# Block 0's Mish loop reordered and block 1's recurrence chain spread over more places, in a fused delta-rule, Mish-MLP and mixture kernel

## The chip, the cores and the metric

One core of a Trainium2 chip runs the whole program. The metric is device microseconds of one execution, the median of a few runs; the time before is 2250.83 us (three runs, 2248.86 to 2260.82).

## The reference, cut to what matters

Three layers follow one another. A delta-rule recurrence runs over 768 positions of 4 batches x 8 heads (head size 48); its output is 3072 tokens of 384 columns. An MLP with 2048 hidden columns and Mish follows, and then a mixture of 8 experts of 1024 hidden columns, weighted by a matrix that eight row and column normalisations balance.

```python
for t in range(S):
    y[:, :, t] = einsum('bhd,bhde->bhe', q[:, :, t], state)
    v_old = einsum('bhde,bhd->bhe', state, k_n[:, :, t])
    state = state + beta * einsum('bhd,bhe->bhde', k_n[:, :, t], v[:, :, t] - v_old)
...
h = x @ w_in;  x = (h * tanh(softplus(h))) @ w_out          # Mish MLP
...
P = exp(x @ w_gate - max); 8 times: P /= rows; P /= columns; P *= N / E
out = sum over e of P[:, e] * (relu(x @ w1[e]) @ w2[e])
```

## The kernel before

Every float32 matrix is split into a high part (fp32r) and a low part, the remainder, so each product is three matmuls: high by high, low by high, high by low.

The first two layers are done in six blocks of 512 tokens (`NBLK`; c is the block). A block has 16 *Mish units*, one for each 128 hidden columns, and blocks 0 and 1 (`c < NE0`) have 8 *expert units* of expert 0 behind them. In Mish unit f TensorE does `m_first` (9 matmuls, line 314, into one of two PSUM buffers), ScalarE does Mish (`m_a`, line 1302 or 1304) and a rounded copy, the high part (`m_c`, line 1310), VectorE or GpSimd subtracts to get the low part (line 1312), and TensorE does `m_second` (9 matmuls, line 1323), two units later. An expert unit is alike with Relu: lines 314, 328, 329 and 338.

Block 0 also decodes the MLP's weights, which arrive as 64-bit words. For each chunk of 128 columns ScalarE does `begin_decode` (line 193, and line 210 in three chunks of four), VectorE does a sign and a shift step (lines 199 and 204; in the fourth chunk line 196 as well), ScalarE rounds to the high part (`rounded`, line 257) and VectorE subtracts (line 276, in `convert`). A weight chunk is then stored to memory, to be loaded again in the next blocks, and its buffer is refilled.

The recurrence of the next block (a *chain*) is woven into the units of this one. Its 64-position triangular systems are inverted in halves: `lane_in` transposes on VectorE, 60 short elimination products and adds on VectorE (lines 1096 and 1102, in the queue `eq`), `st_lane_out` (two transposes, lines 1111 and 1112), matmuls `st_m1` (line 1139) and `st_m2` (line 1154) with copies, and the copies of `st_place` (lines 1121 and 1123). Then come stages z, w, s, y (lines 1181, 1203, 1221, 1237), twice, each with a VectorE or ScalarE step behind it. `st_g` (line 1033) builds the products of the block after the next.

All order is written out by hand, and each engine takes its instructions in that order. The list `MARKS` names the places of a block: s0 to s15 (Mish units), f1 to f4 (the boundary), s16 to s23 (expert units). `PLACES` says where each chain stage goes; `fill(us)` pops eliminations from `eq` until their written costs (0.2 us + size / 960 each) reach `us`; `rate` lets each `vec` instruction pop some too; `drain_elim` does what is left. In blocks from 1 on a place issues its first two stages ahead of the unit's `m_first` and the others behind; in block 0 stages go in pairs ahead of the unit's first product, behind it, and behind its second product.

The other experts run behind the six blocks.

Of the kernel before, what the change touches and what calls it, by code (L numbers as in the profile page):

```python
# [9 lines left out]
F32R = mybir.dt.float32r  # L10
# [75 lines left out]
def delta_mish_sinkhorn_kernel(  # L86
# [137 lines left out]
    def begins(n):  # L224
        while begun[0] < n:
            begin_decode(begun[0])
# [582 lines left out]
    if True:  # L809
# [355 lines left out]
        def m_run(*parts):  # L1165
            for i in range(16):
                for one, _ in parts:
                    one(i)
            return [post for _, post in parts]
# [136 lines left out]
        def m_c(u):  # L1306
            p = hps.pop(u) if u < U1 else mi_x[u % 2]
            h = mi_p.tile([128, 512], F32R, tag="gh", name="gh")
            l = mi_p.tile([128, 512], F32R, tag="gl", name="gl")
            nc.scalar.activation(out=h, in_=p, func=AF.Copy)  # L1310
            eng = nc.vector if u < U1 else nc.gpsimd
            eng.tensor_tensor(out=l, in0=p, in1=h.bitcast(F32), op=ALU.subtract)  # L1312
            gh[u], gl[u] = h, l

# [57 lines left out]
        if True:  # L1372
# [88 lines left out]
            m1a()  # L1461
            warm(2)
            m2a = m_run(st_m2(0, 0, (0,)))[0]
            st_place(0, 0, (0, 2))
            m2a()
            warm(3)
            w = [st_w(0, t) for t in range(2)]
            m1b()
            w[0]()
            m2b = m_run(st_m2(0, 1, (0, 64)))[0]  # L1470
            w[1]()
            s0 = st_s(0, 0)
            m2b()
            warm(1)
            s1 = st_s(0, 1)
            st_place(0, 1, (0, 1, 2, 3))
            s0()
            s1()
            begins(3)
            warm(2)  # L1480
            z = [st_z(0, 2)]
# [40 lines left out]
        def drain_decode():  # L1522
# [2 lines left out]

        two = lambda *marks: [m for m in marks for _ in range(2)]
        PLACES = [
            (22, [24, 24, 24, 24, 24, 24, 25, 25, 25, 25, 25, 25, 26, 26], 16, [26, 26, 27, 27],
             [26, 26, 26, 26, 27, 27, 27, 27], 18, 26, None),
            (8, spread(11, 26, 1, 16), 1, [11, 11, 13, 15], spread(12, 19, 1, 8), 1, 27, 21),  # L1530
        ] + [
            (0, two(3, 5, 7, 8, 9, 11, 12, 13), 0, [3, 3, 6, 7], two(4, 5, 7, 8), 0, 15, 9),
        ] * 4
# [3 lines left out]
        def window(c):  # L1537
# [18 lines left out]
            if nxt < NBLK:  # L1556
                m0, at = PLACES[c][0:2]
                rest[MARKS[m0]].append(drain_elim)
                if c == 0:
                    rest[MARKS[m0]].append(lambda: nc.vector.memset(seed_sb, 0.0))  # L1560
                rest[MARKS[m0]].append(lambda: st_lane_out(nxt))
                if c == 0:
                    rest[MARKS[m0]].append(lambda: nc.gpsimd.memset(seed_sb, 0.0))
                    for t in range(4):
                        rest[MARKS[m0 + t // 2]].append(lambda t=t: prep_v(1, t))
                    for i in range(8):
                        rest[MARKS[m0 + i // 2]].append(lambda t=i // 2, w=1 + i % 2: mask_p(1, t, (w,)))
                if c == 0:
                    m = MARKS[m0 + 1]
                    for make in (st_m1, st_m2):  # L1570
                        for hf in range(2):
                            pe[m].append(lambda hf=hf, make=make: m_run(make(nxt, hf))[0])
                    for hf in range(2):
                        rest[m].append(lambda hf=hf: st_place(nxt, hf, (0, 2)))
                        pe[m].append(lambda t=hf: st_z(nxt, t))
                    ch = [lambda f=f, t=NG * j + g: f(nxt, t) for f, j in (
                        (st_w, 0), (st_s, 0), (st_z, 1), (st_w, 1), (st_y, 0), (st_s, 1), (st_y, 1)
                    ) for g in range(NG)]
                else:
                    for hf in range(2):  # L1580
                        late[MARKS[m0 + 1]].append(lambda hf=hf: m_run(st_m1(nxt, hf))[0])
                        rest[MARKS[m0 + 2]].append(lambda hf=hf: st_place(nxt, hf, (0, 2)))
                        late[MARKS[m0 + 2]].append(lambda hf=hf: m_run(st_m2(nxt, hf))[0])
                    ch = chain_list(nxt)
                assert len(at) >= len(ch)
                for p, stage in zip(at, ch):
                    pe[MARKS[p]].append(stage)
                if c == 0:
                    pe[MARKS[27]][0:0] = [lambda: lambda: None] * 2
# [26 lines left out]
        if True:  # L1616
            banks[:] = [0, [A1, A1]]
            for c in range(NBLK):
# [40 lines left out]
                for f in range(U1 + (3 if c < NE0 else 2)):  # L1659
                    m = MARKS[f]  # L1660
                    posts = side_pe(m, 0)
                    if f < U1:
                        ready(b + f)
                        m_first(b + f)
                        if not c:
                            converts(min(U1, f + 2))
                            if f == 0:
                                for n in (3, 4):
                                    wslots[n] = wpool.tile([128, 2, 2, DM], F32R, tag=f"w{n}", name=f"w{n}")
                            if f == 3:  # L1670
                                wslots.append(late_p.tile([128, 2, 2, DM], F32R, tag="e2", name=f"w{NS1 - 1}"))
                    if 1 <= f <= U1:
                        m_a(b + f - 1)
                        m_c(b + f - 1)
                    if f == 0 and 0 < c <= NE0:
                        y0_second(b - 1)
                    if f == 1 and 0 < c <= NE0:
                        y0_done(c - 1)
                    if f == 5:
                        flush_xr()  # L1680
                    if f == 2 or not c:
                        banks[1] = [A1, A1, (ps_o1, "o3")]
                    if c >= NE0 and split and f >= U1:
                        run(*(split[0:2] if f == U1 else split[2:]))
                    if f == U1 + 1:
                        m_second(b + U1 - 1)
                        x2_done(c)
                    side_rest(m, posts)
                    if 2 <= f <= U1:
                        m_second(b + f - 2)  # L1690
                    fill((0.5 if f < U1 else 2.0) if not c else 3.2 if c >= NE0 and f > 8 else 2.0)
                    if f < U1:
                        if not c:
                            decodes(min(U1, f + 3))
                            if f + 2 < U1:
                                rounded(f + 2)
                            begins(min(U1, f + 4))
                        if ncvt[0] >= U1:
                            conversions(b + f)
                if c >= NE0:  # L1700
                    continue
                side_rest("f4", side_pe("f4", 0))
                fill(2.0)
                banks[1] = [A1, A1]
                for f in range(U1, NU):
                    u = b + f
# [6 lines left out]
                        e_relu(u - 1)  # L1713
                    side_rest(f"s{f}", posts)
                    if f > U1 or not c:
                        fill(2.4 if c == 0 else 3.2)
                    if f > U1 + 1:
                        y0_second(u - 2)
                    if not c:
# [193 lines left out]
```

## Time and profile before

| what | value |
|---|---|
| median of three runs | 2250.83 us |
| the profiled execution: its own time, and its span | 2253.7 us, 2251.9 us |
| TensorE busy | 2169.7 us (96%) |
| VectorE, ScalarE, GpSimd busy | 1394.4, 701.8 and 655.0 us |
| mean granted TensorE clock | 0.98 of full speed |

The busy shares are means over stages with different limits. In the first four of the 40 slices (225 us) TensorE is busy seven tenths, in the next three eight to nine, and the granted clock is below nine tenths in four of these seven; from then on TensorE is busy nine tenths or more. A granted clock of 1.00 is 2.4 GHz and 0.50 is 1.2 GHz; a value between them is a mean over a stretch that had both.

### The profile page before, as it was taken

How to read it: one execution, taken by the hardware profiler on the slowest of the kernel's cores; microseconds unless marked ns; L12 is line 12 of the kernel's file. 1: busy time of each engine (PE TensorE's matmuls, PEld its weight loads, DVE VectorE, ACT ScalarE, POOL GpSimd, SP SyncE). 2: the span in 40 equal slices, each digit the busy share in tenths (PEclk: the TensorE clock that was granted, in tenths of full speed). 3: DMA queues.
4: the chain of work that ended last, by engine and by line, in shares of the span. 5: the costliest groups of instructions: out<-in, count | busy, mean ns of one | idle time of the engine just before them, and what ended most of it. 6: DMA issues, size and time to landing. Idle time of an engine off the chain costs nothing.

```text
span 2251.9 us, 34773 instructions
## 1 busy us (share of the span) xinstructions
PE 2169.7 (96%) x14150; PEld 1788.8 (79%) x14150; DVE 1394.4 (62%) x2296; ACT 701.8 (31%) x1218; POOL 655.0 (29%) x514
## 2 busy tenths in 40 slices
PE   7777989999999999999999999999999999999999
PEld 5656877888888788888888888888888888888887
DVE  7667554655641257777777676666666666666665
ACT  6553332323332445333333322122222222112122
POOL 4104333243422756677878710000000000000000
PEclk8898998999999999999999999999999999999999
DMA  6566542635345535655555435443534454344441
GB/s 183 210 211 202 179 149 100 202 128 188 127 156 197 196 117 198 252 194 194 211 184 213 162 129 157 151 170 125 173 126 146 154 155 157 124 159 135 173 146 47
DMA packets 123648, 370.35 MB, mean 164 GB/s; under 512 B 9440, under 2 KB 51232, under 8 KB 123232
## 3 DMA queue, kind: packets, MB, share of 16 engines
q1 hardware_dynamic: 122912, 367.74, 47.8%
q8 instruction: 111, 1.82, 0.3%
q10 hardware_dynamic: 576, 0.39, 0.1%
q14 instruction: 49, 0.40, 0.1%
HBM read 274.15 MB, written 93.95 MB: 163 GB/s over the span
## 4 chain that ended last, share of the span: by engine, by line
PE 85%; DVE 7%; ACT 2%; issue 2%; POOL 1%; DMA 1%; SPq 0%; DVEq 0%; ACTq 0%; POOLq 0%
PE s L677 33%; PE b L610 30%; PE psh L314 7%; PE x L1323 6%; PE y L338 1%; DVE lane L1102 1%; PE psa L1033 1%; DVE t L1096 1%; PE psa L1181 1%; PE psa L1203 1%; PE psa L1237 1%; PE psa L1154 1%; DVE us L889 1%; PE psa L1139 1%; DVE lane L1066 1%
## 5 line engine op out<-in xcount | busy, mean ns | idle before, releaser
L610 PE MATMUL b<-gx,gw 128*128 128x512 f32 x3036 | 795.3, 390 | 0.1
L617 DVE TENSOR_TENSOR gt<-b,gt 128x512 f32<-128x512 f32 x644 | 435.9, 689 | 459.4 <-PE b L610 429.6
L610 PEld LDWEIGHTS b<-gx,gw 128*128 128x128 f32 x3036 | 568.2, 188 | 118.5 <-ACT gt L619 0.9
L677 PE MATMUL s<-gh,gw 128*128 128x512 f32 x2208 | 622.8, 390 | 1.3 <-DVE gy L720 1.1
L652 ACT ACTIVATE gh<-gt 128x512 fp32r<-128x512 f32 x368 | 232.8, 633 | 933.9 <-DVE gt L646 931.5
L677 PEld LDWEIGHTS s<-gh,gw 128*128 128x128 f32 x2208 | 413.6, 188 | 87.7 <-DVE gy L720 1.5
L677 PE MATMUL s<-gl,gw 128*128 128x512 f32 x1104 | 326.8, 390 | 0.0
L314 PE MATMUL psh<-x,w 128*128 128x512 f32 x1008 | 271.8, 417 | 39.1 <-DVE gl L1312 26.4
L646 DVE SCALAR_TENSOR_TENSOR gt<-gt,gp 128x512 f32<-128x512 f32 x336 | 278.0, 827 | 4.5
L314 PEld LDWEIGHTS psh<-x,w 128*128 128x128 f32 x1008 | 194.2, 199 | 91.1 <-DVE gl L1312 31.8
L677 PEld LDWEIGHTS s<-gl,gw 128*128 128x128 f32 x1104 | 206.9, 188 | 42.8
L655 POOL TENSOR_TENSOR gl<-gt,gh 128x512 fp32r<-128x512 f32 x128 | 185.8, 1458 | 78.5 <-ACT gh L652 71.8
L655 DVE TENSOR_TENSOR gl<-gt,gh 128x512 fp32r<-128x512 f32 x240 | 164.5, 685 | 37.0 <-ACT gh L652 36.8
L1312 POOL TENSOR_TENSOR gl<-x,gh 128x512 fp32r<-128x512 f32 x80 | 102.9, 1288 | 252.1 <-ACT gh L1310 226.4
L1323 PE MATMUL x<-gh,w 128*128 128x512 f32 x576 | 154.6, 405 | 0.7 <-ACT gh L1310 0.7
L550 POOL TENSOR_TENSOR gx<-gxr,gx 128x768 fp32r<-128x768 f32 x18 | 33.3, 1848 | 407.3 <-ACT gx L549 407.3
L481 POOL TENSOR_TENSOR gw<-gr,gw 128x640 fp32r<-128x640 f32 x70 | 117.5, 1681 | 68.2 <-ACT gw L491 66.4
L1323 PEld LDWEIGHTS x<-gh,w 128*128 128x128 f32 x576 | 109.6, 194 | 25.3 <-issue 1.4
L997 POOL TENSOR_TENSOR kq<-kq,mask_sb 64x256 f32<-64x256 f32 (+1 forms) x80 | 67.3, 841 | 77.9 <-ACT kq L992 73.6
L1304 ACT ACTIVATE x<-psh 128x512 f32<-128x512 f32 x80 | 47.6, 596 | 133.5 <-PE psh L314 123.7
L1323 PE MATMUL x<-gl,w 128*128 128x512 f32 x288 | 82.6, 395 | 3.2 <-POOL gl L1312 3.2
L481 POOL TENSOR_TENSOR gw<-raw,gw 128x384 fp32r<-128x384 f32 x70 | 73.4, 1069 | 7.3 <-ACT gw L513 7.3
(206 smaller groups left out, 1946.4 us busy)
## 6 DMA issues: line engine op xcount, KB each, us to landing
gw<-wg SPq DMA_DIRECT2D x57, 1280.0 KB, 8.0
w<-wd SPq DMA_DIRECT2D x88, 768.0 KB, 4.4
gw<-wg SPq DMA_DIRECT2D x57, 768.0 KB, 5.1
wg<-gw SPq DMA_DIRECT2D x29, 1280.0 KB, 6.1
wg<-gw SPq DMA_DIRECT2D x29, 768.0 KB, 5.1
wd<-w SPq DMA_DIRECT2D x24, 768.0 KB, 5.7
gr<-in_w_dram SPq DMA_DIRECT2D x35, 384.0 KB, 3.2
raw<-in_w_dram SPq DMA_DIRECT2D x35, 384.0 KB, 3.6
```

The costliest lines, as they stand in the source:

```text
L314: mm(ps, lhsT=wi(u, pw, kc), rhs=(xh, xl)[px][:, kc, :], start=(n == 0), stop=(n == 3 * KD - 1))
L481: nc.gpsimd.tensor_tensor(out=w[:, 1, lo:hi], in0=r, in1=w[:, 0, lo:hi].bitcast(F32), op=ALU.subtract)
L610: mm(ps, lhsT=w[:, pw, i * 128:i * 128 + 128], rhs=x[:, px, j, :], start=(n == 0), stop=(n == last))
L617: add = lambda o, i: nc.vector.tensor_tensor(out=t[:, o], in0=ps, in1=t[:, i], op=ALU.add)
L646: nc.vector.scalar_tensor_tensor(out=t, in0=t, scalar=0.0, in1=pbs[u, e][:, o:o + 512], op0=ALU.max, op1=ALU.mult)
L652: nc.scalar.activation(out=h, in_=t, func=AF.Copy)
L655: return lambda: eng.tensor_tensor(out=l, in0=t, in1=h.bitcast(F32), op=ALU.subtract)
L677: mm(o[k], lhsT=w[:, pw, at:at + 128], rhs=hids[s, z][ph], start=(start and new and n == 0), stop=(end and not new and n == 2))
L997: nc.gpsimd.tensor_tensor(out=o, in0=o, in1=mask_sb[p, None, :].to_broadcast([64, hs.stop - hs.start, CH]), op=ALU.mult)
L1304: nc.scalar.activation(out=mi_x[u % 2], in_=hps.pop(u), func=AF.Mish)
L1312: eng.tensor_tensor(out=l, in0=p, in1=h.bitcast(F32), op=ALU.subtract)
L1323: mm(x2ps[c][k], lhsT=wo(u, pw, k * 128, k * 128 + 128), rhs=(h, l)[pg], start=(f == 0 and n == 0), stop=(f == U1 - 1 and n == 2))
```

## The change

- Block 0's Mish units: `m_a` and `m_c` of the unit before now come ahead of `converts`, and the `rounded` call at the unit's end is gone, so the rounding of a chunk is issued inside `convert`, one unit later than before.
- Eliminations: block 0 pops 1.0 us a Mish unit (before 0.5), less at the boundary, and none inside `x2_done`; block 1 pops 3.2 a Mish unit (before 2.0) and 2.4 an expert unit (before 3.2).
- Block 1's chain, woven into block 0's expert units: it starts at s16 (before s18) and takes seven places, s17 to s23, two stages at a time.
- Block 1: `st_g` of block 3 two at a time in s12 to s15 (before one at a time in s12 to f4), and block 3's eliminations enter the queue at f1 (before s17). In Mish units 0 to 8 the low part of h is subtracted on VectorE (before GpSimd).
- Start: all four `st_place` copies of the first half on ScalarE (before two on VectorE), and the second half's `st_m2` behind the stages s.

```diff
-            eng = nc.vector if u < U1 else nc.gpsimd
+            eng = nc.vector if u < U1 or place[u][0] == 1 and place[u][1] < 9 else nc.gpsimd
...
-            st_place(0, 0, (0, 2))
+            st_place(0, 0, (0, 1, 2, 3))
             m2a()
             warm(3)
             w = [st_w(0, t) for t in range(2)]
             m1b()
             w[0]()
-            m2b = m_run(st_m2(0, 1, (0, 64)))[0]
             w[1]()
             s0 = st_s(0, 0)
-            m2b()
             warm(1)
             s1 = st_s(0, 1)
             st_place(0, 1, (0, 1, 2, 3))
+            m2b = m_run(st_m2(0, 1, (0, 64)))[0]
             s0()
             s1()
+            m2b()
...
         PLACES = [
-            (22, [24, 24, 24, 24, 24, 24, 25, 25, 25, 25, 25, 25, 26, 26], 16, [26, 26, 27, 27],
-             [26, 26, 26, 26, 27, 27, 27, 27], 18, 26, None),
-            (8, spread(11, 26, 1, 16), 1, [11, 11, 13, 15], spread(12, 19, 1, 8), 1, 27, 21),
+            (20, [22, 22, 23, 23, 23, 23, 24, 24, 24, 24, 24, 24, 25, 25, 26, 26], 16, [24, 25, 26, 27],
+             [25, 25, 25, 25, 26, 26, 27, 27], 18, 26, None),
+            (8, spread(11, 26, 1, 16), 1, [11, 11, 13, 14], two(12, 13, 14, 15), 1, 27, 16),
...
-                        if not c:
-                            converts(min(U1, f + 2))
...
                     if 1 <= f <= U1:
                         m_a(b + f - 1)
                         m_c(b + f - 1)
+                    if not c and f < U1:
+                        converts(min(U1, f + 2))
...
                         m_second(b + U1 - 1)
+                        rate(0.6 if c else 0.0)
                         x2_done(c)
+                        rate(0.6)
...
-                    fill((0.5 if f < U1 else 2.0) if not c else 3.2 if c >= NE0 and f > 8 else 2.0)
+                    if c < NE0:
+                        fill((3.2 if c else 1.0) if f < U1 else 2.0 if f < U1 + 2 else 0.5)
+                    else:
+                        fill(3.2 if f > 8 else 2.0)
                     if f < U1:
                         if not c:
                             decodes(min(U1, f + 3))
-                            if f + 2 < U1:
-                                rounded(f + 2)
                             begins(min(U1, f + 4))
...
-                fill(2.0)
+                fill(0.5)
...
-                        fill(2.4 if c == 0 else 3.2)
+                        fill(2.4)
```

In the code that is left out of the diff, block 0's `st_m1` moves to place s17 and its `st_m2` to s18, with `st_place` beside `st_m1`, and the stage z of the first pair becomes part of the list that `PLACES` places.

## Rows read from the trace of the kernel before

**Rows 1.** Windows by stage of blocks 0 and 1: stretch, length, busy us per engine (instructions), PEclk, DMA share.

```profile
68.49:178.12 109.63, 82.51 (x354) 62.05 (x352) 71.69 (x107) 55.88 (x85) 1.90 (x2) 0.89 0.65 225
178.12:263.87 85.75, 69.92 (x1089) 61.03 (x1089) 51.03 (x99) 25.48 (x50) 38.49 (x38) 0.90 0.53 178
263.87:303.17 39.30, 37.39 (x168) 30.64 (x166) 34.99 (x67) 14.19 (x25) 17.15 (x10) 1.00 0.69 216
303.17:318.26 15.09, 10.51 (x151) 8.80 (x152) 8.96 (x17) 4.80 (x8) 1.28 (x1) 0.66 0.20 67
...
360.96:375.89 14.93, 12.83 (x170) 11.24 (x169) 5.07 (x10) 5.93 (x14) 7.52 (x10) 0.66 0.30 107
375.89:419.26 43.37, 40.70 (x348) 36.21 (x344) 35.97 (x86) 6.26 (x11) 0.00 (x0) 0.96 0.43 145
419.26:2251.90 1832.64, 1817.73 (x10236) 1502.62 (x10233) 1126.94 (x1779) 527.32 (x849) 535.41 (x400) 1.00 0.47 161
```

**Rows 2.** Waits of TensorE from 0 to 430 us: total us, times, longest.

```profile
PE psh L314 <- DVE gl L1312: 26.4, 13, 4.5
PE psh L314 <- DVE hl L329: 8.2, 1, 8.2
PE psa L1154 <- issue: 6.1, 3, 4.3
PE psa L1139 <- DVE t L1111: 5.2, 3, 4.6
```

**Rows 3.** Timeline of one Mish unit of block 0: start, us, engine, line, instruction.

```profile
96.28 0.95 DVE L199 SCALAR_TENSOR_TENSOR kq<-kq 128x768 int32<-128x768 int32 x1
...
97.27 0.96 DVE L204 SCALAR_TENSOR_TENSOR kq<-kq 128x768 int32<-128x768 int32 x1
...
98.26 0.89 ACT L257 ACTIVATE w<-kq 128x768 fp32r<-128x768 f32 x1 [5.28 <-DVE kq L204]
99.05 0.91 ACT L193 ACTIVATE kq<-kq 128x768 f32<-128x768 f32 x1
99.18 0.96 DVE L276 TENSOR_TENSOR w<-kq,w 128x768 fp32r<-128x768 f32 x1 [0.95 <-ACT w L257]
99.83 0.90 ACT L210 ACTIVATE kq<-kq 128x768 int32<-128x768 uint16 x1
...
100.59 0.62 ACT L1302 ACTIVATE psh<-psh 128x512 f32<-128x512 f32 x1
...
101.24 0.60 ACT L1310 ACTIVATE gh<-psh 128x512 fp32r<-128x512 f32 x1
101.87 0.69 DVE L1312 TENSOR_TENSOR gl<-psh,gh 128x512 fp32r<-128x512 f32 x1 [1.74 <-ACT gh L1310]
...
102.89 0.95 DVE L199 SCALAR_TENSOR_TENSOR kq<-kq 128x768 int32<-128x768 int32 x1
```

**Rows 4.** Timeline of VectorE late in block 0's Mish units.

```profile
163.22 0.56 DVE L196 TENSOR_SCALAR kq<-kq 128x768 int32<-128x768 int32 x1
...
166.72 0.96 DVE L276 TENSOR_TENSOR w<-kq,w 128x768 fp32r<-128x768 f32 x1 [0.96 <-ACT w L257]
```

**Rows 5.** Chain of waits, 305 to 323 us: start, us, what.

```profile
305.59 2.02 DVE t L1111
...
311.38 4.14 PE x L1323 x9
...
320.40 2.26 PE x L1323 x9
```

**Rows 6.** Timeline of VectorE, block 3's `lane_in` in block 1's expert units.

```profile
381.04 3.98 DVE L1066 STREAM_TRANSPOSE lane<-gx 32x1024 f32<-32x1024 f32 x2
```

**Rows 7.** Timeline of GpSimd in block 1's Mish units.

```profile
289.08 1.28 POOL L1312 TENSOR_TENSOR gl<-x,gh 128x512 fp32r<-128x512 f32 x1 [2.32 <-ACT gh L1310]
```

**Rows 8.** Timeline of VectorE beside rows 7.

```profile
289.21 1.42 DVE L1102 TENSOR_TENSOR lane<-lane,t 128x238 f32<-128x238 f32 x1
290.66 0.41 DVE L1096 TENSOR_TENSOR t<-lane 128x240 f32<-128x240 f32 x1
```

More of the change, by code (lines that the diff above doesn't have):

```diff
@@ L1568, in window @@
                 if c == 0:
[L1569 to L1572, printed above, removed]
                     for hf in range(2):
-                        rest[m].append(lambda hf=hf: st_place(nxt, hf, (0, 2)))
-                        pe[m].append(lambda t=hf: st_z(nxt, t))
+                        pe[MARKS[m0 + 1]].append(lambda hf=hf: m_run(st_m1(nxt, hf))[0])
+                        rest[MARKS[m0 + 1]].append(lambda hf=hf: st_place(nxt, hf, (0, 2)))
+                        pe[MARKS[m0 + 2]].append(lambda hf=hf: m_run(st_m2(nxt, hf))[0])
+                    pe[MARKS[m0 + 2]].extend([lambda: lambda: None] * 2)
                     ch = [lambda f=f, t=NG * j + g: f(nxt, t) for f, j in (
-                        (st_w, 0), (st_s, 0), (st_z, 1), (st_w, 1), (st_y, 0), (st_s, 1), (st_y, 1)
+                        (st_z, 0), (st_w, 0), (st_s, 0), (st_z, 1), (st_w, 1), (st_y, 0), (st_s, 1), (st_y, 1)
                     ) for g in range(NG)]
@@ L1664, in delta_mish_sinkhorn_kernel @@
                         m_first(b + f)
-                        if not c:
-                            converts(min(U1, f + 2))
[L1667 to L1671, printed above, removed]
                     if 1 <= f <= U1:
@@ L1674, in delta_mish_sinkhorn_kernel @@
                         m_c(b + f - 1)
+                    if not c and f < U1:
+                        converts(min(U1, f + 2))
+                        if f == 0:
+                            for n in (3, 4):
+                                wslots[n] = wpool.tile([128, 2, 2, DM], F32R, tag=f"w{n}", name=f"w{n}")
+                        if f == 3:
+                            wslots.append(late_p.tile([128, 2, 2, DM], F32R, tag="e2", name=f"w{NS1 - 1}"))
                     if f == 0 and 0 < c <= NE0:
```

## The prediction, made before the changed kernel ran

> **What bounds the kernel now.** I read the windows by stage first. From 419 us on, 1832.64 us of the span, TensorE is busy 1817.73 us at a clock of 1.00 [rows 1], and the edits touch nothing there; whatever this change does, it does in the first 419 us. In block 0's Mish units TensorE is busy 82.5 of 109.6 us at a mean clock of 0.89, in block 0's expert units 69.9 of 85.8 at 0.90, and two short stretches in block 1 (303 to 318 and 361 to 376 us) stand at 0.66 [rows 1]. No other engine is full over either of the first two, so there it is a loop of waits that sets the pace.
>
> Next I read TensorE's waits. The largest is 26.4 us in 13 pieces for the low part of h (line 1312), then one wait of 8.2 for an expert unit's low part, 6.1 in three pieces inside `st_m2` with no releaser, 5.2 for the turn (line 1111), of which 4.6 in one piece [rows 2]. Block 1's expert units idle 2.7 us (40.70 of 43.37 busy [rows 1]).
>
> Last the timeline of one unit. VectorE's shift ends at 98.23, ScalarE rounds at 98.26 (line 257), then decodes the next chunk (193, 210), then does Mish (1302 at 100.59) and the high part (1310 at 101.24); VectorE, idle 1.74 us, subtracts at 101.87, does two eliminations, and starts the next sign step at 102.89 [rows 3]. From sign step to sign step that is 6.61 us, and every link is on the path: the rounding stands on ScalarE ahead of two decodes and of Mish, so VectorE's line 1312 waits for all of them, and the next decode steps stand behind it. The eliminations grow, so late units take longer: line 276 for chunk 5 ends at 100.14 [rows 3], for chunk 15 at 167.68 [rows 4], 67.5 us for ten chunks.
>
> **Block 0's Mish units.** Now Mish and the high part go first on ScalarE and the rounding follows them. When VectorE's shift ends, the high part is already there; line 1312 (0.69) runs while ScalarE rounds. From the end of the shift to line 276 it is still 0.95 us (98.23 to 99.18); then 0.96 for line 276, the eliminations, 0.99 from sign to shift and 0.96 for the shift [rows 3]. Of eliminations `fill(1.0)` pops three in most units; their written costs sum to 1.05 to 1.35, and the largest takes 0.41 where 0.45 is written [rows 8], so I take 1.05. Sum: 0.95 + 0.96 + 1.05 + 0.99 + 0.96 = 4.91, and 0.56 more in each fourth chunk [rows 4]. Ten chunks: 49.1 + 3 x 0.56 = 50.8 where they took 67.5, so 16.7 us less. ScalarE's round is 0.79 + 0.78 + 0.76 + 0.65 + 0.63 = 3.6 us from start to start [rows 3], and TensorE's two products are 4.5 (nine matmuls in 2.26 at full clock [rows 5]); both lie inside 4.91. The first units have the same loop, but a 2 us transpose and other chain work on VectorE besides; there I take 1.1 us for each of four units, between 0 and the 1.74 that line 1312 waits. In sum **-21** (-15 to -24). A refill of a buffer has two such periods less one rounding, some 9 us, to land; memory moves 225 GB/s in this stage at 0.65 of the DMA engines' time [rows 1], and the same bytes in 88 us ask for 280, so I cost the DMAs at nothing. Were that cover gone, ScalarE's line 193 would wait.
>
> **Block 0's expert units.** The 8.2 us [rows 2] are VectorE popping 2.0 + 2.0 + 2.0 + 2.4 us of eliminations between `x2_done` and the first expert low part. Now more are done before; by the written costs 3.5 us are left behind `x2_done`, and none is popped between its three subtractions. But the turn (2.02 [rows 5], and its second transpose of about the same length) moves up to s16, ahead of that low part, and `st_m1` stands at the head of s17 and needs the first of the two. From the end of the Mish products: 3.3 for the three subtractions behind the last pops, 1.7 for a copy and the sums of squares, 3.5 and 2.0: the turn is done after some 11 us, TensorE's first expert product after 4. It waits 7 us in place of 8.2: the stall stays and changes its name to line 1111. What goes is the 4.3 us hole inside `st_m2` [rows 2], because a whole product now stands between `st_m1` and `st_m2`. Its cause is not shown, so its worth lies between 0 and 4.3; I take 3.5, since the wait is not tied to an operand. With stages two at a time, each with a product of 2.3 us ahead of its consumer, the chain adds no wait that I can find. 1.2 + 3.5 + about 1.3 from the undisturbed subtractions: **-6** (-1 to -12, the latter if the new wait is short enough to keep the clock).
>
> **Block 1's Mish units.** VectorE is busy 35.0 of 39.3 us [rows 1]. Each low part on GpSimd holds a VectorE add up: 1.42 us where its neighbour takes 0.41 [rows 7, 8]. So moving eight low parts costs VectorE 8 x 0.69 and returns about 7 x 1.0: nothing net. The three `lane_in` transposes (2.0 each [rows 6]), 22.3 of eliminations by written cost, 5.5 of low parts and some 5 (an estimate) of copies, sums and norms make 39 us from 265.4, where VectorE has the last low part of x done, 1.5 us into the stage; the turn's first half then ends at 306.4, 1.2 us before its present 307.6 [rows 5]. `drain_elim` at s8 then finds nothing, and TensorE, which had one wait of 4.6 us [rows 2], meets several of up to 2 us at `m_second`, whose low parts stand behind larger fills. The gain is the clock: in 303 to 318 us (0.66) 15.1 us go to 4.6 of waiting and to work of 6.8 at full clock, so 3.7 are lost to half speed; nine matmuls take 4.14 there and 2.26 later [rows 5]. In the stage ahead TensorE was busy 37.4 of 39.3 us at 1.00 [rows 1], so short waits do not lower it. -1.2 - 3.7, and some 0.6 of the 1.9 that TensorE idles in the stage ahead: **-5.5** (0 to -8.3).
>
> **Boundary and expert units of block 1.** Four `st_g` move ahead of `x2_done`, the same TensorE work earlier. One 2 us transpose of block 3 is now popped between `x2_done`'s subtractions; ScalarE's last copy to xr waits for these, the y copies stand behind it, and a stage z needs their PSUM buffer. That takes what the shorter boundary returns: **0** (-3 to +3). In the expert units the transposes (6.0 us [rows 6]) no longer stand ahead of a low part: the 2.7 us go, and one product at half speed (about 1.5; clock 0.96 in this stage [rows 1]): **-4** (-5 to -1).
>
> **Start.** The two `st_place` copies leave VectorE, so its copy of the first half's `st_m2`, and stage w behind that, come 0.65 us sooner; of the three holes in `st_m2` the two here sum to 1.8 us (6.1 less 4.3 [rows 2]), and the second half's `st_m2` with its hole no longer stands ahead of stage s. **-2** (0 to -2.5).
>
> **Sum.** -21 - 6 - 5.5 + 0 - 4 - 2 = -38.5. The profiled execution took 2253.7 us, so 2215.2; it lies 2.9 above the median of the runs, so I predict **2212**.
>
> **The rivals.** (a) The Mish loop closes less far, at some 6 us a chunk: a refill lands later than its 9 us under the heavier traffic and line 193 waits, as a 26% higher rate would bring if landings stretch. For it: the engines have stretches at full use inside the 0.65 mean. Against: it needs landings twice as long as the traffic now shows. Then -9 in place of -21: 2224. (b) VectorE is what block 1 runs into: the larger fills put the low parts late in every unit, some 0.7 us in each of the first nine, and the clock falls all the same: -5.5 becomes +3, and 2220. For it: 35.0 of 39.3 busy already. (c) The stall in the expert units shrinks below what lowers the clock, and the half-speed products there (clock 0.90 over 85.8 us [rows 1]) go as well: -12 there, 2206. (d) The other side: TensorE stays at 1.2 GHz through block 0's Mish units. In this stage the clock is 0.89 [rows 1] with a wait in nearly every unit; a unit at half clock costs 2 x 4.14 = 8.3 us [rows 5] in place of 4.9, so each such unit takes 3.4 back, and from twelve of the sixteen on the kernel is slower than before; with all sixteen, 54 back: 2266. Against: the stage ahead of 303 us, with TensorE busy 95%, is at 1.00, and the new loop leaves it busy over 85%.
>
> On (d) the Trainium skill (TensorE: Matmul & The Clock Gate, What's actually happening) holds that the low clock is the default and that activity releases it; by that rule a loop with idle time in every unit might stay low, which is case (d). That the stage now has 0.89 with TensorE three quarters busy speaks against it.
>
> **How the numbers follow.** The likeliest case has 0.50, (a) 0.17, (b) 0.13, (c) 0.18, (d) 0.02. The range that leaves out no more than two in ten reaches from (c), with its bounds added, to past (a): 2198 to 2230. A change of 0.5% is 11 us, about what a measurement of this kernel can tell from none: 2239.6 is passed only by (d) or by (a) and (b) together with the small ends of the other bounds, so faster has 0.95, the same 0.04, slower 0.01.
>
> **What would show it.** In the profile after, line 276 comes every 4.9 us, line 1312 follows the shift with no wait, and the 26.4 us wait on it is nearly gone; block 0's Mish stage is some 88 us long at a clock near 1.00. A wait of some 7 us stands at line 1139 for line 1111, and no hole of 4 in line 1154. In block 1 no wait over 2.5 us up to the chain, and no stretch at half clock there. The forecast is wrong if line 193 waits for a DMA, if `m_second` waits in every unit of block 1, or if the new wait at `st_m1` grows beyond 10.

## The result, and the profile after

The changed kernel takes 2223.4 us (median of four runs, 2216.5 to 2225.1) where the kernel before took 2250.25 beside it: a ratio of 0.9865, with a 95% interval of 0.983 to 0.990. The profiled executions differ by 30.1 us (2253.7 and 2223.6), where the sum of the prediction was 38.5. The median is 11.4 us above the 2212 that was forecast: 8.4 are missing from the sum, and the rest comes from the profiled execution of before, which lay 2.9 above its median, where this one lies at it.

The windows by stage of the changed kernel, with cuts at the same events as in [rows 1] (first product of block 0's Mish units; end of its last x2 product; first product of block 1; end of block 1's last x2 product; first expert product; first product of block 2; end):

```profile
core 0: us, PE busy (x) PEld busy (x) DVE busy (x) ACT busy (x) POOL busy (x), PEclk, DMA share, GB/s
67.33:155.17 87.84, 75.67 (x354) 55.50 (x352) 76.59 (x123) 56.11 (x85) 1.90 (x2) 0.98 0.80 280
155.17:241.13 85.96, 71.40 (x1089) 63.14 (x1089) 47.36 (x84) 25.56 (x50) 39.58 (x38) 0.88 0.49 169
241.13:333.30 92.17, 90.55 (x913) 71.78 (x913) 57.05 (x114) 34.07 (x64) 33.52 (x32) 1.00 0.55 176
333.30:339.88 6.58, 3.34 (x97) 3.07 (x97) 6.12 (x14) 3.01 (x7) 0.00 (x0) 0.97 0.11 45
339.88:383.69 43.81, 43.81 (x387) 38.66 (x385) 29.15 (x76) 6.86 (x12) 0.00 (x0) 0.97 0.52 176
383.69:2221.80 1838.11, 1821.97 (x10236) 1505.95 (x10234) 1125.79 (x1779) 527.63 (x849) 536.04 (x400) 0.99 0.47 161
```

Beside the marks of the kernel before (68.49, 178.12, 263.87, 360.96, 370.67, 419.26, 2251.9):

| stretch | before | after | difference | predicted |
|---|---|---|---|---|
| up to the first Mish unit | 68.49 | 67.33 | -1.2 | -2 |
| Mish units, block 0 | 109.63 | 87.84 | -21.8 | -21 |
| expert units, block 0 | 85.75 | 85.96 | +0.2 | -6 |
| Mish units, block 1 | 97.09 | 92.17 | -4.9 | -5.5 |
| boundary, block 1 | 9.71 | 6.58 | -3.1 | 0 |
| expert units, block 1 | 48.59 | 43.81 | -4.8 | -4 |
| all behind | 1832.64 | 1838.11 | +5.5 | 0 |

Two of the seven terms fail: block 0's expert units, and the long rest that no edit touches. The boundary's -3.1 is at the edge of its range. In block 0's Mish units the loop runs as worked out (timeline of VectorE and ScalarE, one unit; columns as in [rows 3]):

```profile
97.51 0.68 DVE L1312 TENSOR_TENSOR gl<-psh,gh 128x512 fp32r<-128x512 f32 x1
98.56 0.96 DVE L276 TENSOR_TENSOR w<-kq,w 128x768 fp32r<-128x768 f32 x1 [0.37 <-ACT w L257]
100.64 0.60 ACT L1310 ACTIVATE gh<-psh 128x512 fp32r<-128x512 f32 x1
102.80 0.68 DVE L1312 TENSOR_TENSOR gl<-psh,gh 128x512 fp32r<-128x512 f32 x1
102.92 0.90 ACT L257 ACTIVATE w<-kq 128x768 fp32r<-128x768 f32 x1 [1.68 <-DVE kq L204]
103.85 0.96 DVE L276 TENSOR_TENSOR w<-kq,w 128x768 fp32r<-128x768 f32 x1 [0.37 <-ACT w L257]
```

The high part at 100.64 is ready 1.6 us before VectorE subtracts at 102.80; the rounding runs beside that, and line 276 follows 0.4 us later. This unit, with a fourth-chunk step, takes 5.29 us. Line 276 ends at 94.6 us for chunk 5 and at 145.4 for chunk 15: ten chunks in 50.8 us, which is the figure of the prediction's sum, where they took 67.5.

TensorE's longest waits in block 0's expert units:

```profile
engine line waited for: us in total, times, longest us
PE psa L1139 <- DVE t L1111: 6.9, 1, 6.9
PE psa L1181 <- DVE gx L889: 3.4, 1, 3.4
PE psa L1203 <- issue: 1.9, 1, 1.9
```

The first, for the turn (lines 1111 and 1112), is the stall renamed, at the size forecast (7). The other two the prediction did not have: a wait in stage z, and a hole with no operand to wait for, which is gone from `st_m2` and stands in a stage w.

### The profile page after: what moved, and what is told of

Same layout as the page of the kernel before. It is cut to its first block, busy times and chain, and to the rows that moved or that the text cites. A ratio compares the mean times of both kernels' runs of the same rounds, so it can differ in the third digit from the quotient of the medians.

```text
span 2221.8 us, 34776 instructions
## 1 busy us (share of the span) xinstructions
PE 2162.9 (97%) x14150; PEld 1781.3 (80%) x14150; DVE 1390.5 (63%) x2303; ACT 703.6 (32%) x1220; POOL 645.2 (29%) x505
## 4 chain that ended last, share of the span: by engine, by line
PE 87%; DVE 8%; DMA 2%; ACT 1%; issue 1%; POOL 0%; SPq 0%; DVEq 0%; ACTq 0%; POOLq 0%
PE s L677 34%; PE b L610 31%; PE psh L314 8%; PE x L1323 6%; DVE t L1096 2%; DVE lane L1102 2%; PE y L338 1%; PE psa L1033 1%; PE psa L1203 1%; PE psa L1181 1%; PE psa L1154 1%; PE psa L1237 1%; PE psa L1139 1%; DVE w L276 1%; ACT w L257 1%
## 5 line engine op out<-in xcount | busy, mean ns | idle before, releaser
L314 PEld LDWEIGHTS psh<-x,w 128*128 128x128 f32 x1008 | 188.8, 193 | 68.2 <-DVE w L276 10.8
L1312 POOL TENSOR_TENSOR gl<-x,gh 128x512 fp32r<-128x512 f32 x71 | 91.5, 1290 | 253.1 <-ACT gh L1310 239.5
L481 POOL TENSOR_TENSOR gw<-gr,gw 128x640 fp32r<-128x640 f32 x70 | 117.5, 1682 | 68.0 <-ACT gw L491 66.2
```

The lines of the kernel that those rows point to most:

```text
L314: mm(ps, lhsT=wi(u, pw, kc), rhs=(xh, xl)[px][:, kc, :], start=(n == 0), stop=(n == 3 * KD - 1))
L481: nc.gpsimd.tensor_tensor(out=w[:, 1, lo:hi], in0=r, in1=w[:, 0, lo:hi].bitcast(F32), op=ALU.subtract)
```

## The experiments

All stages below are cut at the events named above. Every ratio is to the kernel before on the same chip; medians of different lines were partly taken on different chips (the kernel before took 2246.6 to 2255.2 there), so ratios are what is compared. Columns M0, E0, M1, B1, E1 are Mish, expert, Mish, boundary and expert units of blocks 0, 0, 1, 1, 1 in the one profiled execution.

| run | median | ratio (95%) | M0 | E0 | M1 | B1 | E1 | rest |
|---|---|---|---|---|---|---|---|---|
| after, again | 2222.1 | 0.9867 (0.984-0.989) | 87.73 | 85.65 | 92.18 | 6.64 | 43.76 | 1839.05 |
| loop order alone | 2219.8 | 0.9863 (0.983-0.989) | 81.51 | 81.56 | 95.98 | 9.80 | 48.50 | 1831.75 |
| places on ScalarE | 2217.7 | 0.9854 (0.983-0.988) | 87.83 | 77.20 | 92.23 | 7.25 | 44.34 | 1833.49 |
| inverses behind product | 2215.2 | 0.9838 (0.981-0.986) | 87.79 | 80.05 | 92.18 | 6.45 | 43.99 | 1832.69 |
| old window of block 0 | 2212.0 | 0.9844 (0.983-0.986) | 81.74 | 80.39 | 92.21 | 7.25 | 44.32 | 1832.64 |
| fill 0.5 in M0 | 2220.1 | 0.9878 (0.986-0.990) | 81.61 | 90.60 | 92.21 | 7.02 | 44.89 | 1836.67 |
| low parts on GpSimd | 2225.0 | 0.9908 (0.989-0.993) | 88.11 | 80.95 | 96.64 | 6.51 | 43.89 | 1832.80 |
| none popped in x2_done | 2217.2 | 0.9865 (0.985-0.988) | 87.61 | 86.43 | 92.20 | 4.23 | 43.45 | 1830.85 |
| fill 2.0 in M1 | 2225.0 | 0.9868 (0.984-0.990) | 87.75 | 85.73 | 95.73 | 6.53 | 43.88 | 1832.08 |
| late pops | 2210.9 | 0.9809 (0.978-0.984) | 81.65 | 84.57 | 92.17 | 4.33 | 43.85 | 1836.13 |
| late pops, places | 2209.5 | 0.9802 (0.978-0.983) | 81.87 | 80.59 | 92.17 | 4.24 | 43.47 | 1839.95 |
| old window, places | 2203.9 | 0.9799 (0.977-0.983) | 82.02 | 79.76 | 92.19 | 4.23 | 43.94 | 1833.24 |

**1. The changed kernel again** (no edit).

> The changed kernel itself, profiled a second time. Theory: the 5.5 us that its first profile loses behind the start of block 2 belong to that one execution. There TensorE has a hole of 2.31 us without an operand in line 314 at 495 us (1.02 us in the profile before) and a wait of 1.77 for a weight at 736 us (1.29 before), each followed by products at half clock. Then a second profile has a hole of another length or none at these places, and takes some 4 to 6 us less behind block 2's start; block 0's Mish units again take 87.8 us within 1. Rival: the loss belongs to the change, since every transfer now starts some 35 us sooner and meets others: the same two places with the same lengths within 0.3 us.

The theory falls. The matmuls behind the hole, in the first profile of the changed kernel and in the second:

```profile
497.32 1.22 PE L314 MATMUL psh<-x,w 128*128 128x512 f32 x2 [2.31 <-issue]
```

```profile
501.88 0.50 PE L314 MATMUL psh<-x,w 128*128 128x512 f32 x1 [2.31 <-issue]
```

The same hole of 2.31 us comes back, and the rest is 1839.05 long. The rival does not hold as it stands either, since the wait for a weight is 2.5 us here and 1.8 in the first profile. The hole is there, 2.0 to 2.7 us, in all twelve runs, and the rest takes from 1830.85 to 1839.95 in them, with the same instructions in it. What separates long from short is the granted clock behind the hole. These are the 10 us that begin 4 us behind its end, in the changed kernel and in the last run of experiment 7, whose hole is 2.31 us as well (columns as in the windows above):

```profile
501.32:511.32 10.00, 10.00 (x194) 8.59 (x195) 3.57 (x8) 2.40 (x4) 1.27 (x1) 0.56 0.07 18
```

```profile
486.02:496.02 10.00, 10.00 (x221) 8.73 (x221) 4.95 (x13) 3.00 (x5) 1.27 (x1) 1.00 0.23 80
```

In this stretch the clock is 1.00 in the eight runs whose rest takes 1830.85 to 1833.49 us, and 0.55 to 0.65 in the four with 1836.13 to 1839.95 us. So the loss is neither an accident of one execution nor the hole alone; what decides how long the half-clock stretch behind the hole lasts is open.

**2. The loop order alone, in the kernel before.**

```diff
+                    if 1 <= f <= U1:
+                        m_a(b + f - 1)
+                        m_c(b + f - 1)
                     if not c and f < U1:
                         converts(min(U1, f + 2))
...
-                            if f + 2 < U1:
-                                rounded(f + 2)
```

> The kernel before with one part of the change: Mish and the high part ahead of the rounding in block 0's Mish units; its fills of 0.5, its places and all else stay. Theory: the rounding ahead of Mish is the whole cause of the 26.4 us wait. VectorE's loop is 0.95 + 0.96 + two eliminations of some 0.35 + 0.99 + 0.96 = 4.6 us a chunk, next to TensorE's 4.5, so these units take 83 to 87 us in place of 109.6, and block 0's expert units stay near 86 with the 8.2 us wait for the low part. In all 22 to 26 us less than the kernel before. Rival: the larger fill or the earlier transposes are needed for the loop to close: period near 6 us, stage above 97 us, gain below 13.

One part of the change gives all of its time: 0.9863 against 0.9867. Its windows (M0, E0, then M1):

```profile
67.70:149.21 81.51, 73.89 (x354) 55.79 (x352) 70.63 (x107) 56.15 (x85) 1.90 (x2) 0.98 0.84 301
149.21:230.77 81.56, 70.82 (x1088) 61.91 (x1089) 50.95 (x99) 25.61 (x50) 39.46 (x38) 0.90 0.56 189
230.77:326.75 95.98, 91.30 (x881) 74.10 (x881) 52.65 (x100) 31.77 (x58) 38.03 (x31) 0.95 0.50 161
```

The theory holds and is too small: M0 is 28.1 us shorter than before and E0 4.2, though its places and its `st_m2` right behind `st_m1` are as before; the hole of 4.3 us is gone all the same. Against this run the whole change is 10.7 us slower over block 0 (173.8 to 163.1) and 11.7 faster over block 1's three stages (142.6 to 154.3).

**3. Fills of 0.5 in block 0's Mish units of the changed kernel.**

```diff
-fill((3.2 if c else 1.0) if f < U1 else ...
+fill((3.2 if c else 0.5) if f < U1 else ...
```

> The changed kernel with fills of 0.5 in place of 1.0 in block 0's Mish units, all else as it is. Theory: VectorE sets the pace of these units, so an elimination there costs its full length: VectorE was busy 70.6 us with fills of 0.5 (loop order alone) and 76.6 with 1.0, and the stages differ by 6.3. So this stage falls to 81 to 82 us, and the eliminations come back ahead of the turn, whose wait grows from 6.9 us to about 13; with the clock falling in it, block 0's expert units grow by 6 to 9. In sum 0 to 3 slower. Rival: the eliminations left over find idle VectorE time in f1 to f4 and the wait for the turn grows by less than 2: 4 to 6 us faster.

The theory holds: M0 falls by 6.2 us to 81.6, and the turn is that much later (waits of E0):

```profile
PE psa L1139 <- DVE t L1111: 13.5, 1, 13.5
PE psa L1181 <- DVE gx L889: 1.8, 1, 1.8
```

M0 and E0 together are 172.2, against 173.4 and 173.8. An elimination costs the same in the loop, which VectorE paces, as ahead of the turn. What the larger fill buys is a turn that stands two places earlier, and that does not earn its price here: experiment 7 begins with a run that has neither, and M0 and E0 take 162.1 us together.

**4. The copies of the diagonal blocks on ScalarE; the inverses behind the product.**

```diff
-rest[MARKS[m0 + 1]].append(lambda hf=hf: st_place(nxt, hf, (0, 2)))
+rest[MARKS[m0 + 1]].append(lambda hf=hf: st_place(nxt, hf, (0, 1, 2, 3)))
```

> The changed kernel with all the copies of the diagonal blocks (line 1123) in block 0's expert units on ScalarE in place of half of them on VectorE. Theory: in the changed kernel stage z waits 3.4 us for VectorE's copies of the second product, since four of VectorE's copies of diagonal blocks take 4.7 us there beside GpSimd's masks (2.7 without them, at 285 us); without them the copies come 3 to 4 us sooner, the wait falls below 1, and block 0's expert units go from 86.0 to 81 to 83 us, more if the half-clock stretch behind it goes too. Rival: ScalarE takes over as the one that is late, or the rounding and VectorE's line 276 are what z waits for anyway: the stage stays within 1.5 us of 86.

First the changed kernel's timeline ahead of its wait in stage z:

```profile
172.61 8.52 POOL L997 TENSOR_TENSOR kq<-kq,mask_sb 64x512 f32<-64x512 f32 x6
173.95 4.68 DVE L1123 COPY gx<-yd 32x512 f32<-32x512 f32 x4
181.33 0.96 DVE L276 TENSOR_TENSOR w<-raw,w 128x768 fp32r<-128x768 f32 x1
182.20 0.68 DVE L329 SCALAR_TENSOR_TENSOR hl<-psh,hh 128x512 fp32r<-128x512 f32 x1
182.80 1.37 DVE L889 COPY gx<-psa 32x512 f32<-32x512 f32 x2
184.32 0.22 PE L1181 MATMUL psa<-us,kq 48*64 48x48 f32 x1 [3.44 <-DVE gx L889]
...
284.68 2.73 DVE L1123 COPY gx<-yd 32x512 f32<-32x512 f32 x4
```

The four copies take 4.68 us beside GpSimd's masks and 2.73 in block 1, where GpSimd has one low part beside them. A copy that starts while GpSimd is idle takes 0.42 us; the three beside the masks take 1.41 each, and the one beside the low part 1.43. The second triangle product ended at 175.86; VectorE's copies of it begin at 182.80. In the experiment:

```profile
179.80 0.94 DVE L276 TENSOR_TENSOR w<-raw,w 128x768 fp32r<-128x768 f32 x1
180.66 0.68 DVE L329 SCALAR_TENSOR_TENSOR hl<-psh,hh 128x512 fp32r<-128x512 f32 x1
181.26 1.37 DVE L889 COPY gx<-psa 32x512 f32<-32x512 f32 x2
```

Its start was 3.2 us later, so these copies come 4.8 us sooner against the stage; the wait at z and the hole behind it are gone, TensorE runs at 1.00 from z on, and E0 is 77.2, 8.8 us less (forecast: 3 to 5, and more if the half-clock stretch went too, as it did). How much of that the copies are worth by themselves is less sure. Of five executions with block 0 unedited, four have E0 at 85.65 to 86.43, and one (low parts on GpSimd, experiment 5) has 80.95, without a wait at z; against that one the edit is worth 3.8 us. The Trainium skill's page SBUF — State Buffer (Who interferes with whom) says that a VectorE copy can need the ports it shares with GpSimd, and that the later of the two then waits. The 1.41 and 1.43 against 0.42 agree with it.

The inverses behind the product:

```diff
-                        rest[MARKS[m0 + 1]].append(lambda hf=hf: st_place(nxt, hf, (0, 2)))
+                        rest[MARKS[m0 + 2]].append(lambda hf=hf: st_place(nxt, hf, (0, 2)))
...
+                    for m in (m0 + 1, m0 + 2):
+                        pe[MARKS[m]][0:0] = [lambda: lambda: None] * 2
```

> The changed kernel with both triangle products of block 0's expert units set behind the expert product of their unit in place of ahead of it, and the copies of the diagonal blocks one unit later. Theory: the 6.9 us wait for the turn is a wait of TensorE with 2.3 us of other work standing right behind it; done first, it leaves 4.6 us of waiting, and the stage is 2.3 us shorter, or 4 if the next products then keep the clock. Rival: what stands behind the turn (copies, second product, stage z) moves back by the same product, and the wait at z grows from 3.4 to over 5: the stage stays within 1 us or grows.

The wait for the turn is 4.2 in place of 6.9, with 1.3 more for the copy of the first product; z waits 1.4. E0 is 80.05, but the 80.95 with block 0 unedited stands against it, so this gain is not told apart from the spread of E0.

**5. Block 1's first low parts on GpSimd again; fills of 2.0 there.**

```diff
-eng = nc.vector if u < U1 or place[u][0] == 1 and place[u][1] < 9 else nc.gpsimd
+eng = nc.vector if u < U1 else nc.gpsimd
```

> The changed kernel with block 1's first nine low parts of h on GpSimd again. Theory: moving them is worth nothing by itself, as each costs VectorE 0.69 us and a low part on GpSimd holds one VectorE add up by some 1.0: block 1's Mish units stay within 1.5 us of 92.2. Rival: with the larger fills VectorE has no slack, a low part of 1.5 us on GpSimd comes later than one of 0.7 on VectorE, and TensorE waits in several units: the stage grows by 3 us or more.

The rival holds, by another way than it names. VectorE, GpSimd and TensorE around the low parts of units 2 and 3 of block 1:

```profile
250.84 1.00 DVE L922 TENSOR_REDUCE ss<-sq 128x8 f32<-128x384 f32 x2
251.93 5.46 POOL L938 TENSOR_TENSOR ne<-ss,half_sb 128x32 f32<-128x32 f32 x1 [6.60 <-DVE ss L922]
257.36 2.79 POOL L1312 TENSOR_TENSOR gl<-x,gh 128x512 fp32r<-128x512 f32 x2
258.80 0.80 PE L1323 MATMUL x<-gl,w 128*128 128x512 f32 x1 [4.59 <-POOL gl L1312]
```

GpSimd's power (line 938) takes 5.46 us, and a low part queued behind it makes TensorE wait 4.6 us, once. In the kernel before the same queue cost 1.9 us:

```profile
PE x L1323 <- POOL gl L1312: 1.9, 1, 1.9
```

There the sums (line 922) began 12.2 us into the stage, here 14.7, since larger fills stand ahead of them on VectorE. The fills do the same with the low parts on VectorE: 15.0 us in the changed kernel, 13.3 in the next run, with fills of 2.0.

```diff
-fill((3.2 if c else 1.0) if f < U1 else ...
+fill((2.0 if c else 1.0) if f < U1 else ...
```

> The changed kernel with fills of 2.0 in place of 3.2 in block 1's Mish units, low parts on VectorE as changed. The run with the low parts back on GpSimd took 96.6 us in block 1's Mish units, with a wait of 4.6 us for a low part, where the changed kernel takes 92.2. Theory: the gain there comes from VectorE's low parts alone, and the larger fill adds nothing: 92 to 93 us. Rival: without the larger fill eliminations are left for the drain ahead of the turn, which comes later; the wait of over 3 us for the turn (line 1111) is back, with products at half clock behind it: 95 us or more.

The rival holds, and M1 is 95.7, with this wait of TensorE:

```profile
PE psa L1139 <- DVE t L1111: 3.3, 1, 3.3
```

So the larger fill alone leaves 96.6 and the low parts alone 95.7, where block 1 as it was took 97.1 and, in experiment 2, 96.0; both together give 92.2.

**6. Nothing popped between block 1's three subtractions.**

```diff
-                        rate(0.6 if c else 0.0)
+                        rate(0.0)
```

> The changed kernel with no elimination or transpose popped between the three subtractions of block 1 either. Theory: at the boundary of block 1 TensorE waits 3.2 us for the y copy, which stands on ScalarE behind the last copy to xr, which waits for VectorE's three subtractions, of which two are held up by a transpose of 1.93 us; without it the wait is some 1.3 us, the boundary goes from 6.6 to some 4.6 us, and the half-clock product behind it may go too (another 1.3). The transpose finds room later on VectorE. Rival: it lands ahead of the first expert low part instead, and block 1's expert units grow by as much.

The theory holds. VectorE and ScalarE at the boundary, in the changed kernel and in the experiment:

```profile
333.51 0.69 DVE L889 TENSOR_TENSOR x<-x,x 128x512 fp32r<-128x512 f32 x1 [0.70 <-ACT x L1330]
334.24 1.93 DVE L1066 STREAM_TRANSPOSE lane<-gx 32x1024 f32<-32x1024 f32 x1
336.19 0.69 DVE L889 TENSOR_TENSOR x<-x,x 128x512 fp32r<-128x512 f32 x1
337.64 0.60 ACT L1338 ACTIVATE xr<-x 128x512 f32<-128x512 f32 x1 [2.69 <-DVE x L889]
338.14 0.87 ACT L1239 ACTIVATE yd<-psa 128x384 f32<-128x384 f32 x2
```

```profile
333.89 1.89 DVE L889 TENSOR_TENSOR x<-x,x 128x512 fp32r<-128x512 f32 x3 [0.69 <-ACT x L1330]
335.81 0.60 ACT L1338 ACTIVATE xr<-x 128x512 f32<-128x512 f32 x1 [0.49 <-DVE x L889]
336.30 0.87 ACT L1239 ACTIVATE yd<-psa 128x384 f32<-128x384 f32 x2
336.40 1.94 DVE L1066 STREAM_TRANSPOSE lane<-gx 32x1024 f32<-32x1024 f32 x1
```

The wait for the y copy goes from 3.2 to 1.0, B1 from 6.6 to 4.2, and E1 does not grow.

**7. Block 0's window as before, with all of block 1's edits, and three versions of it.** `PLACES[0]`, the chain's code for block 0 and block 0's fills are those of the kernel before; the new loop order stays.

> The changed kernel with block 0's window as it was before (turn at s18, the chain's seven stages in its old places, fills of 0.5 and 2.0, eliminations between the three subtractions); the new order in the Mish units, the edits of the start and all of block 1's edits stay. Theory: the run with the loop order alone took 81.5 us in block 0's Mish units and 81.6 in its expert units where the changed kernel takes 87.8 and 86.0, so the larger fill and the new places cost 10.7 us there, and block 1's edits are worth 12 by themselves: stages of 81.5, 81.6, 92.2, 6.6 and 43.8 us, a span near 2205, some 11 to 15 us less than the changed kernel's. Rival: block 1 gains only because block 0's window hands it a chain that is further along: then block 1's three stages take 97, 10 and 48 us again, as in the kernel before, and the span stays near 2217.

The theory holds in every stage within 1.2 us (81.7, 80.4, 92.2, 7.3, 44.3): block 1's edits keep their worth without block 0's. By its ratio the run is not told apart from the changed kernel. The span is 2208.8, as this execution reached the first Mish unit only at 70.25 us. Then the pops of block 0 moved behind its first expert low part, without and with the copies on ScalarE:

```diff
-fill((3.2 if c else 0.5) if f < U1 else 2.0 if f < U1 + 2 or not c else 0.5)
+fill((3.2 if c else 0.5) if f < U1 else (2.0 if f < U1 + 2 else 0.5) if c else 1.0 if f == U1 else 0.0)
...
-fill(0.5 if c else 2.0)
+fill(0.5 if c else 0.0)
...
-fill(2.4)
+fill(2.4 if c else 3.2)
...
-rate(0.6)
+rate(0.0)
```

> The kernel with block 0's window as before and the other edits of the change, in which block 0 pops its eliminations later: 1.0 at f1, none at f2 to f4 and none between the three subtractions (nor in block 1's), and 3.2 in place of 2.4 in each expert unit. With the old window TensorE waits 7.0 us for the first expert low part, which stands on VectorE behind some 8 us of eliminations, and VectorE then idles 2.7 us ahead of the turn. Theory: the low part comes first, the wait falls below 2, the eliminations fill the idle time of the next two units, the turn comes no later, and block 0's expert units take 74 to 77 us in place of 80.4; block 1's boundary takes 4.3 in place of 7.3. Rival: the eliminations left to the drain make the turn late instead, and TensorE waits 5 to 7 us there: the stage stays within 2 us of 80.4.

> The same, with all copies of the diagonal blocks (line 1123) of block 0's expert units on ScalarE. Theory: as in the changed kernel, these copies beside GpSimd's masks keep VectorE from the copies that stage z waits for; without them block 0's expert units are 1 to 3 us shorter than without this edit. Rival: in the old places TensorE waits only 1.1 us at z, so nothing is to be had: within 1 us.

E0 grows to 84.6: the low part is waited for 3.7 us and the turn 6.1, where one wait of 7.0 stood, so the rival is right and too mild. With the copies on ScalarE E0 is 80.6, 4.0 less, but not by way of z, where neither run waits. The first half of the turn ends 21.8 us into the stage in both; it is waited for 3.6 us in place of 6.1, as TensorE comes to it later, having run more of the work ahead of it at half clock (mean clock 0.64 in place of 0.80 in the 12 us ahead). The 16 us from the end of that wait on, in the two runs:

```profile
170.35:186.35 16.00, 16.00 (x283) 14.76 (x283) 11.05 (x12) 5.71 (x9) 15.39 (x14) 0.52 0.33 126
```

```profile
171.14:187.14 16.00, 16.00 (x412) 14.85 (x412) 8.73 (x12) 9.56 (x15) 15.39 (x14) 0.80 0.34 126
```

So the 4.0 us lie in where the half-clock stretches fall, and no run shows that the copies moved them. The last run keeps the old fills:

> The kernel with block 0's window as before and the other edits of the change, nothing popped between the subtractions of either block, and all copies of the diagonal blocks in block 0's expert units on ScalarE; the fills of block 0's window are those of before (2.0, 2.4). Theory: each part keeps what it showed alone: 81.7 us for block 0's Mish units, 78 to 80 for its expert units, 92.2, 4.3 and 43.5 for block 1's three stages; the span is 2203 to 2207, of which some 3 us hang on how long the clock stays low behind the hole in block 3. Rival: block 0's expert units hang on the one wait for the low part and the half-clock products behind it, whatever follows; they stay at 80.4 or above, and only block 1's boundary brings 3 us: 2206 to 2212.

It has the lowest median: 2203.9 us, 0.980 of the kernel before (0.977 to 0.983), an interval that overlaps those of the two versions with late pops. E0 fell only to 79.8 from 80.4: the wait at z of 1.1 us is gone, and more the copies cannot bring in the old places. Block 1's boundary brings 3.0.

## Why the prediction was right, and where it was wrong

**Block 0's Mish units (-21; -21.8).** Right in mechanism and size, and the fill was priced rightly at its length in VectorE's loop. What the prediction did not draw from its own sum is that the loop would close at some 81.5 us without the larger fill. Rival (a), refills that land late, did not come. The traffic rose to 280 GB/s (301 with the loop order alone), and the median landing of the two refills from 3.9 and 4.5 us to 5.4 and 6.0, still inside the 9 us of cover: line 193 waits for no DMA. TensorE's waits on lines 276 and 257 are 1.6 us at most, 11.0 in all. Rival (d) did not come: the clock is 0.98 in this stage. By the rule of the Trainium skill that was weighed with it (TensorE: Matmul & The Clock Gate, What's actually happening), that the low clock is the default and activity releases it, the loop might have stayed low; the granted clock says that it did not.

**Block 0's expert units (-6; +0.2).** This term failed. The renamed stall was right (6.9), and with it rival (c) did not come: the clock in this stage is 0.88. "What goes is the 4.3 us hole inside `st_m2`" was wrong in its reason: experiment 2 leaves the two products together and has no hole, the changed kernel has one of 1.9 in a stage w. The hole was not the order's to remove, and its cause stays open. "The chain adds no wait that I can find" was wrong: the prediction counted TensorE's work between a stage and its consumer, and not VectorE's queue between them, which held four copies (4.68 us, lengthened by GpSimd's masks), the norms, line 276 and a low part. Experiment 4 shows that the copies make z late. The chain's stages also stand closer than the section on the change says: in six places, s17 to s22, and not in seven. The length of the stage also depends on where the half-clock stretch falls. Windows of the changed kernel from the turn on, and of the run with the low parts on GpSimd, whose block 0 is the same:

```profile
166.03:173.00 6.97, 6.97 (x138) 6.21 (x139) 4.44 (x5) 4.54 (x7) 6.82 (x9) 0.55 0.49 173
173.00:184.30 11.30, 7.88 (x162) 7.12 (x161) 10.30 (x14) 3.22 (x5) 10.50 (x9) 1.00 0.08 21
184.30:197.00 12.70, 10.79 (x151) 9.67 (x153) 4.89 (x10) 0.84 (x1) 1.46 (x2) 0.60 0.78 297
```

```profile
166.05:182.40 16.35, 16.35 (x283) 14.51 (x283) 11.74 (x15) 7.15 (x11) 14.79 (x15) 0.51 0.21 76
182.40:197.00 14.60, 14.60 (x283) 13.57 (x282) 11.05 (x21) 2.04 (x3) 3.76 (x4) 1.00 0.74 279
```

In both VectorE gives stage z its operand at about the same time (184.2 and 184.6). In the first TensorE was back at full clock shortly before 173, came early, waited 3.4 us and then ran at 0.60. In the second it ran slowly for as long as VectorE needed for the operand, did not wait, and ran the rest at 1.00. E0 is 5.0 us shorter.

**Block 1's Mish units (-5.5; -4.9).** The size is right, as is the end of the half-clock stretch (0.66 before [rows 1], 1.00 now); one step is wrong. "Moving eight low parts ... nothing net" (the edit moves nine) held for VectorE's time, 38.8 us busy in the first 42 us of the stage with the move and without it, but the move takes the low parts out of the queue behind GpSimd's power: without it M1 is 4.5 us longer. The row for it was in the trace of before (experiment 5): the wait of 1.9 us, of which the prediction gave back 0.6. Rival (b) did not come: the waits for VectorE's low parts sum to 1.5 us.

**Boundary and expert units of block 1 (0 and -4; -3.1 and -4.8).** Two of the moved `st_g` (1.1 us each) now stand ahead of the x2 end and lengthen M1, so -0.9 of the -3.1 is the boundary's own and block 1's Mish units gained 7.1. The popped transpose costs what was written: without it (experiment 6) the boundary is 2.4 us shorter. In the expert units the 2.7 us of idle time went, as forecast, and the rest is the clock, 0.92 before and 0.97 after.

**Start (-2; -1.2).** Not told: the twelve runs and the changed kernel reach the first Mish unit at 66.2 to 70.6 us, and the run with the old start at 67.7.

**The rest (0; +5.5).** "The edits touch nothing there" is right of the instructions and wrong of the time. It took the length of the half-clock stretches there as fixed; the runs part by the one behind the hole of experiment 1, and their spread of 9 us should have been in the range's bounds.

## What to carry to other kernels

When a chain is moved, count the queue of every engine between a stage and its consumer, with what runs beside it on GpSimd, and not TensorE's cover alone. Where an engine paces a loop, work moved into that loop is paid in full, so it must buy something later; run the one part of a change that carries its gain by itself, since here the other parts summed to next to nothing (10.7 us lost in block 0, 11.7 won in block 1). A small operation behind a long one on GpSimd costs its queue, not its own length.

## What the runs showed of the hardware

A TensorE hole with no operand to wait for, of 2.0 to 2.7 us, stands at one product of block 3 in all twelve runs and was 1.02 before; no run here settles its cause. Execution of the same instructions from block 2 on takes 1830.85 to 1839.95 us, and TensorE's busy time moves with it (1817.7 us of 1832.64 before [rows 1], 1822.0 of 1838.11 after), so most of that difference is work at the lower clock. A half-clock stretch costs little where another engine sets the pace, and time where TensorE does (the two sets of windows of block 0's expert units above, with E0 5.0 us apart).

A VectorE copy of 32x512 in SBUF takes 0.42 us alone, 1.41 beside GpSimd's products of 64x512 and 1.43 beside its subtraction of 128x512. GpSimd's power of 128x32, which takes 5.43 us in the changed kernel, holds up none of VectorE's adds and products beside it: they take 0.36 to 0.41 us there.
